# A fused attention, mixture-of-experts and gated product kernel: the last stage's token pairs taken from neighbouring columns, and its first operands formed during the last experts

## The chip, the cores and the metric

The kernel runs on one core of a Trainium2 chip. The metric is the time of one execution on the device in microseconds (us), and the time given is the median of several runs. The engines are named as in the profile: PE is TensorE (matmuls), ACT is ScalarE, DVE is VectorE, POOL is GpSimd, and SP is SyncE, which here only issues DMAs.

## The reference

The weights of the last stage are float64 in memory; tokens are the 4 x 448 = 1792 rows of `x`, with 768 features.

```python
# attention, 4 x 12 heads of 448 x 64, with q and k normalised
x = attn_out.transpose(0, 2, 1, 3).reshape(1792, 768)
# experts: each token goes to the one expert (of 8) with the largest logit
h = np.maximum(x[mask] @ w1[e], 0.0)           # 768 -> 1024
out[mask] = gate_w[mask, None] * (h @ w2[e])   # 1024 -> 768
# gated product
a = x @ moe2_w1                                # 768 -> 1024
b = x @ moe2_w2
h = a * b @ w3                                 # 1024 -> 1024
return h @ w_out                               # 1024 -> 768
```

## The kernel before

**Attention and routing** come first, to about 455 us of the span. The product of `w3` and `w_out` is formed there too. The tokens are then scattered in the order of their experts to `bk` in DRAM by POOL's indirect DMAs, seven for `bk` and fourteen small ones for `md`.

**Experts.** The eight experts run one after the other, the one with the most tokens first (room for `CAP` = 320, 288, 272, 256, 240, 224, 208, 192 tokens). SP reads each expert's number into a register (`value_load`, L781), then issues the loads of its weights (`st`, L666 and L672) and tokens (`xr` for the first expert, `xte` for the others). ACT and DVE split each weight block into an fp16 high part and an fp16 rest (`split`, L659 and L660: `w1t`, `w2t`), and PE multiplies in three terms (`mm3`, L683: high by high, low by high, high by low). Results go to columns of `y32`, six blocks of 128 features by token, three by DVE (`result`, L720) and three by ACT (L722), at a column that comes from a register. Ahead of expert 5 (`LR`) stands a loop for tokens beyond `CAP` (`overflow`, L771), which is not entered here but is a branch on every engine.

**Gated product.** `a` and `b` (called z = 0 and 1) are formed by a seven-product form of a 2 x 2 block multiplication. One of the two splits is over tokens: a column c1 of `y32` is paired with a column c2. The features split into blocks 0 to 2 and 3 to 5, which gives the four parts b11, b21, b12, b22 of the tokens. From them come seven operands, B11, B21, B22 and the differences T1 to T4, each split in two fp16 parts (`operands`, L856 on ACT and L857 on DVE, tile `b`). The tokens are treated in two pieces (s = 0, 1) of two times 448 columns: c1 = s*448, c2 = 896 + s*448. The differences go to temporaries (`t`, L868 to L875), on DVE for s = 0 and on POOL for s = 1.

The weights have seven combinations too (`combos`): for each of four column groups fp, z and three blocks j, a DMA, three DVE instructions that make fp32 of float64 (`from64`, L124 to L126, tile `y32w`), four sums on POOL (L821 to L824) and a split on ACT and DVE (`m2w`, L659 and L660). The sets (0,0), (0,1) and (1,0) of (fp, z) are written ahead of `operands(0)`. `half(fp, s)` issues 2 x 7 products of nine matmuls each for one column group and piece; in all 1008 matmuls. DVE adds up the results (L907, L909, tiles `u`, `ua`, `ub`, `c`), DVE and POOL multiply a by b, and ACT and POOL split the product into `ab`.

**Last product and scatter.** `ab` times the product of `w3` and `w_out` (L983, tile `pso`, 672 matmuls of 384 columns), then a scatter to `out` by POOL.

The order on each engine comes from a scheduler that simulates the program, from the order in which it is written; an instruction waits for its inputs and for its tile to come free, and everything behind it on its engine waits with it.

Of the kernel before, what the change touches and what calls it, by code (L numbers as in the profile page):

```python
# [44 lines left out]
def fused_kernel(ctx, tc, q, k, v, g_q, g_k, w_gate, w1, w2, m_w1, m_w2, m_w3, m_wo, out):  # L45
# [603 lines left out]
    mid = ctx.enter_context(ExitStack())  # L649
    stg = pools(mid)("stg", STG)  # L650
    xtp = pools(mid)("xtp", 2)
    w2p = pools(mid)("w2p", 9)
    ext = pools(mid)("ext", 1)
    htp = pools(mid)("htp", 2)
    ycv = pools(mid)("ycv", 2)
    y32 = yp.tile([P, 6, NT + CW], F32, name="y32")
# [76 lines left out]
    def expert(xt, w, ca, cd):  # L733
        n = xt.shape[2]
        ht = htp.tile([P, 8, 2, CW], F16, tag="ht", name="ht")[:, :, :, 0:n]
# [42 lines left out]

    for r in range(NE):
# [12 lines left out]
        if r == LR:  # L792
            overflow()
        with ExitStack() as order:
            if r < IAR:
                order.enter_context(tc.issue_after(marks["xt"].ins))
            wb += blk
        if r:
            ca = nc.scalar.value_load(srti[0:1, 2, r:r + 1], min_val=0, max_val=NT)
            cd = nc.vector.value_load(srti[0:1, 2, r:r + 1], min_val=0, max_val=NT)  # L800
        expert(xt, wb, ca, cd)
# [4 lines left out]
    HT = NT // 2  # L806
    SN = HT // 2
    SB = 4

    def combos(fp, z, j, staging, conv):  # L810
# [5 lines left out]
        y = conv.tile([P, 8, P], U32, tag="y", name="y32w")  # L816
# [17 lines left out]
    for fp, z in ((0, 0), (0, 1), (1, 0)):  # L834
        weights(fp, z, stg, ycv)
    mid.close()
    two = ctx.enter_context(ExitStack())
    bp = pools(two)("bp", 1)
    tp = pools(two)("tp", 8)
    prep2 = two.enter_context(ExitStack())  # L840
    dst = pools(prep2)("dst", 2)
    ycv2 = pools(prep2)("ycv2", 2)
    S1, S2, S3, S4, A12, A22, A11 = range(7)
    T1, T2, T3, T4, B11, B21, B22 = range(7)
    bt = [[bp.tile([P, 2, HT], F16, name=f"b{o}_{j}") for j in range(3)] for o in range(7)]

    def temp(name):
        return tp.tile([P, SN], F32, tag="t", name=name)

    def operands(s):  # L850

        c1, c2 = slice(s * SN, (s + 1) * SN), slice(HT + s * SN, HT + (s + 1) * SN)
        tt = nc.vector.tensor_tensor

        def put(o, j, x):
            nc.scalar.activation(bt[o][j][:, 0, c1], x, AF.Copy)  # L856
            tt(bt[o][j][:, 1, c1], x, bt[o][j][:, 0, c1], op=ALU.subtract)  # L857

        for j in range(3):
            put(B11, j, y32[:, j, c1])  # L860
        for j in range(3):
            put(B21, j, y32[:, j + 3, c1])
        e = tt if s == 0 else nc.gpsimd.tensor_tensor
        last = []
        for j in range(3):
            b11, b21, b12, b22 = y32[:, j, c1], y32[:, j + 3, c1], y32[:, j, c2], y32[:, j + 3, c2]
            t1, t2 = temp("t1"), temp("t2")
            e(t1, b12, b11, op=ALU.subtract)  # L868
            e(t2, b22, t1, op=ALU.subtract)
            put(T2, j, t2)  # L870
            put(T1, j, t1)
            e(t2, b21, t2, op=ALU.subtract)
            put(T4, j, t2)
            t3 = temp("t3")
            e(t3, b22, b12, op=ALU.subtract)  # L875
            put(T3, j, t3)
            put(B22, j, b22)

    def product(ps, w, a, o, s, first, last=True):
        cs = slice(a * P, (a + 1) * P)  # L880
        c1 = slice(s * SN, (s + 1) * SN)
        mm3(ps, [(w[j][:, 0, cs], w[j][:, 1, cs], bt[o][j][:, 0, c1], bt[o][j][:, 1, c1]) for j in range(3)], first, last,
            skip_group_check=not first)

    ab = []

    def half(fp, s):

        stt, tt = nc.vector.scalar_tensor_tensor, nc.vector.tensor_tensor
        c1, c2 = slice(s * SN, (s + 1) * SN), slice(HT + s * SN, HT + (s + 1) * SN)  # L890
        r = 1.0 / 256
        u = [temp("ua"), None]
# [3 lines left out]
        def begin(z):  # L896
            ps = bank(SN)
            product(ps, wst2[fp, z], A11, B11, s, True, True)
            if z:
                u[1] = temp("ub")  # L900
# [10 lines left out]
        def rest(z):  # L911
            w = wst2[fp, z]
            ps = bank(SN)
            product(ps, w, S2, T2, s, True, True)
            add(u[z], ps, u[z], z)
            ps = bank(SN)
            product(ps, w, S3, T3, s, True, True)
            t1 = temp("u3")
            add(t1, ps, u[z], z)
            product(ps, w, A22, T4, s, False, True)  # L920
            x21 = temp("c21")
            add(x21, ps, u[z], z)
            ps = bank(SN)
# [12 lines left out]
        a11 = temp("a11")  # L936
# [3 lines left out]
        yield  # L940
        done(0, 0, a11)
        a = rest(0)
        b = rest(1)
        for k in ((1, 0), (1, 1), (0, 1)):
# [4 lines left out]
    operands(0)  # L949
    h = half(0, 0)  # L950
    next(h)
    operands(1)
# [4 lines left out]
    for f in range(8):  # L957
        ab.append(abp.tile([P, 2, NT], F16, name=f"ab{f}"))
    next(h)
    for fp in range(SB):  # L960
        for s in range(2):
# [3 lines left out]
            if s == 0 and fp < SB - 1:  # L965
                weights(fp + 1, 1, dst, ycv2)
            if s == 0 and fp < SB - 2:
                weights(fp + 2, 0, dst, ycv2)
# [6 lines left out]
    order = (0, 1, 2, 7, 8, 9, 3, 4, 5, 6, 10, 11, 12, 13)  # L975
    for col in order:
# [35 lines left out]
```

## Time and profile before

| what | value |
|---|---|
| median of 3 runs | 1105.84 us (1104.05 to 1112.1) |
| profiled execution | 1105.45 us |
| its span | 1103.4 us |
| mean granted TensorE clock | 0.922 of full speed |
| PE, DVE, ACT, POOL busy | 84%, 58%, 41%, 36% of the span |

The span is what the trace covers, from the first instruction to the last; the execution's time is 2 us longer. A clock of 1.00 means the higher of TensorE's two levels, 2.4 GHz, and 0.50 the lower, 1.2 GHz. "Busy" counts only the time in which an engine executes; the busy share of PE hides whether a matmul ran at the full or the half clock.

### The profile page before, as it was taken

To read this page: it belongs to the slowest core of one execution; us is meant where nothing else is said; L and a number is where in the kernel's file an instruction comes from. 1 tells how busy PE (TensorE), PEld (TensorE's weight loads), DVE (VectorE), ACT (ScalarE), POOL (GpSimd) and SP (SyncE) were. 2 spreads that over 40 slices of the span, in tenths; PEclk is the share of its full clock that TensorE was granted. 3 is DMA by queue.
4 is the path that set the end of the run, shared out by engine and by line. 5 is a ranking of instruction groups with operands and counts; after the bars stand their busy time and mean duration, and the time that the engine had idled before them with its cause. 6 is when DMAs were issued, how large, how long until landed. Compare 5 with 4: busy or idle time off the path is not lost. (4 is left out here: it accounts for less than half of the span.)

```text
span 1103.4 us, 19950 instructions
## 1 busy us (share of the span) xinstructions
PE 932.0 (84%) x7963; PEld 616.1 (56%) x7963; DVE 637.4 (58%) x952; ACT 447.2 (41%) x651; POOL 392.7 (36%) x530
## 2 busy tenths in 40 slices
PE   1657899998878879539999998893869999999997
PEld 1224466555545557317778898893425555556664
DVE  5948647677846872247554564768975776420000
ACT  3435546576736661035443454642622232210000
POOL 6826244445552441510000000015575665431111
PEclk9876699999979989859999999997869999999999
DMA  6775454333243664368666747861111211121111
GB/s 183 250 243 157 112 118 105 96 89 88 52 147 93 166 153 99 129 210 254 229 182 179 236 159 214 289 227 61 39 39 39 77 58 39 43 72 43 58 46 56
DMA packets 159569, 141.56 MB, mean 128 GB/s; under 512 B 93344, under 2 KB 137904, under 8 KB 159472
## 3 DMA queue, kind: packets, MB, share of 16 engines
q1 hardware_dynamic: 152256, 126.06, 40.1%
q0 software_dynamic: 2864, 11.04, 2.6%
q10 hardware_dynamic: 4352, 3.15, 0.9%
q8 instruction: 63, 1.03, 0.4%
q14 instruction: 34, 0.28, 0.1%
HBM read 98.28 MB, written 22.03 MB: 109 GB/s over the span
## 5 line engine op out<-in xcount | busy, mean ns | idle before, releaser
L683 PE MATMUL psm<-b,m2w 128*128 128x448 f16 x1008 | 201.0, 362 | 32.1 <-ACT b L856 20.4
L683 PEld LDWEIGHTS <-m2w 128*128 128x128 f16 x1008 | 100.4, 100 | 132.1 <-issue 41.4
L683 PE MATMUL psm<-ht,w2t 128*128 128x320 f16 (+7 forms) x1152 | 127.8, 272 | 7.3 <-DVE ht L715 3.9
L683 PE MATMUL psm<-xte,w1t 128*128 128x320 f16 (+7 forms) x1152 | 126.3, 272 | 2.4 <-PEq L771 2.4
L683 PEld LDWEIGHTS <-w2t 128*128 128x128 f16 x1152 | 110.2, 99 | 23.6 <-issue 9.2
L683 PEld LDWEIGHTS <-w1t 128*128 128x128 f16 x1152 | 109.7, 99 | 17.8 <-issue 2.6
L821 POOL TENSOR_TENSOR y32w<-y32w 128x128 f32<-128x128 f32 x24 | 14.2, 592 | 289.6 <-DVE y32w L126 286.7
L288 DVE TENSOR_REDUCE nm<-psm 128x2 f16<-128x896 f32 x84 | 90.7, 1083 | 36.5 <-PE psm L287 36.1
L983 PE MATMUL pso<-ww,ab 128*128 128x384 f16 x672 | 109.7, 326 | 0.0
L336 PE MATMUL po<-vf,e 128*128 128x65 f32 (+1 forms) x480 | 90.8, 288 | 2.7 <-issue 2.7
L983 PEld LDWEIGHTS <-ab 128*128 128x128 f16 x672 | 65.8, 98 | 43.6
L660 DVE SCALAR_TENSOR_TENSOR w2t<-st,w2t 128x768 f16<-128x768 f32 x64 | 60.2, 955 | 47.7 <-ACT w2t L659 47.4
L287 PE MATMUL psm<-kh,qh 64*64 64x448 f16 x336 | 55.4, 409 | 31.7 <-DVE nm L288 19.6
L339 PE MATMUL po<-v,e 128*128 128x65 f16 (+1 forms) x528 | 77.9, 200 | 4.5 <-DVE x L350 2.6
L341 PE MATMUL po<-v,e 128*128 128x65 f16 (+1 forms) x528 | 76.8, 196 | 2.1 <-issue 2.1
L340 PE MATMUL po<-vl,e 128*128 128x64 f16 (+1 forms) x528 | 77.5, 197 | 1.2 <-issue 1.2
L336 PEld LDWEIGHTS po<-vf,e 128*128 128x128 f32 (+1 forms) x480 | 67.9, 191 | 11.4 <-issue 10.8
L339 PEld LDWEIGHTS <-e 128*128 128x128 f16 (+1 forms) x528 | 59.6, 118 | 22.7 <-issue 14.8
L660 DVE SCALAR_TENSOR_TENSOR w1t<-st,w1t 128x1024 f16<-128x1024 f32 x48 | 58.1, 1222 | 22.1 <-ACT w1t L659 21.9
L317 ACT ACTIVATE pss<-pss,ln 128x896 f32<-128x896 f32 x54 | 52.7, 977 | 44.0 <-PE pss L308 38.2
L659 ACT ACTIVATE w2t<-st 128x768 f16<-128x768 f32 x64 | 52.0, 838 | 37.7 <-DMA st<-in_moe_w_dram 33.2
L987 DVE TENSOR_SCALAR ob<-pso,meta_s 128x384 f32<-128x384 f32 x14 | 8.7, 618 | 98.2 <-PE pso L983 98.2
(232 smaller groups left out, 1745.4 us busy)
## 6 DMA issues: line engine op xcount, KB each, us to landing
st<-in_moe_w_dram SPq DMA_DIRECT2D x48, 512.0 KB, 4.9
st<-in_moe_w_dram SPq DMA_DIRECT2D x64, 384.0 KB, 4.0
st<-in_moe_w_dram SPq DMA_DIRECT2D x48, 256.0 KB, 3.4
w<-in_moe_w_dram SPq DMA_DIRECT2D x16, 512.0 KB, 4.0
bk<-zero SPq DMA_DIRECT2D x8, 960.0 KB, 11.6
w<-in_moe_w_out_dram SPq DMA_DIRECT2D x16, 384.0 KB, 3.6
xrow<-rx SPq DMA_DIRECT2D x12, 448.0 KB, 4.5
kf<-in_k_dram SPq DMA_DIRECT2D x24, 192.0 KB, 3.1
```

Of the source, the lines that this page charges most:

```text
L287: nc.tensor.matmul(ps[h, z, 0:S], lhsT=s["q"][0][h, c:c + 64], rhs=s["k"][0][h, S * j:S * j + S], start=True, stop=True)
L288: nc.vector.tensor_reduce(s["nm"][:, t], ps[:, :, 0:S], axis=AX.X, op=ALU.max, negate=True)
L317: nc.scalar.activation(p, p, AF.Exp, bias=ln16, scale=SCL)
L336: nc.tensor.matmul(ov[r, t, :], lhsT=e[0], rhs=vfs[i % 2][:, h, c, 0:D + 1], start=z == 0, stop=z == 3)
L339: nc.tensor.matmul(ov[r, t, :], lhsT=e[0], rhs=vh, start=z == 0, stop=False)
L340: nc.tensor.matmul(ov[r, t, 0:D], lhsT=e[0], rhs=s["vl"][:, h, c, :], start=False, stop=False)
L341: nc.tensor.matmul(ov[r, t, :], lhsT=e[1], rhs=vh, start=False, stop=z == 3)
L659: nc.scalar.activation(dst[:, 0], src, AF.Copy, scale=scale)
L660: nc.vector.scalar_tensor_tensor(dst[:, 1], src, scale, dst[:, 0], op0=ALU.mult, op1=ALU.subtract)
L683: nc.tensor.matmul(ps, lhsT=x, rhs=y, start=first and j == 0, stop=last and j == n - 1, **kw)
L821: e(s1, a21, a22, op=ALU.add)
L983: nc.tensor.matmul(pp[z], lhsT=ab[f][:, x, ts], rhs=ww[f][:, y, z * 384:(z + 1) * 384], start=f == 0 and x == 0 and y == 0, stop=f == 7 an ...
```

## The change

**Token pairs.** The pieces are now `PC = ((0, 384), (768, 512))`: piece 0 pairs columns 0 to 383 with 384 to 767, piece 1 pairs columns 768 to 1279 with 1280 to 1791. The first piece so needs only the tokens of the first experts.

**Operands.** `operands(s)` works on three feature blocks at once (3 x 384 or 3 x 512 elements), with one tile for each operand. The differences are made in place in `y32`, all on DVE. It is a generator: four steps of `operands(0)` are written behind expert 5 and the others behind expert 6, and `operands(1)` is stepped between the products of `half(0, 0)`.

**Weights.** Only the sets (0,0) and (0,1) are written ahead of the gated product. (1,0) and all later ones put their fp32 combinations into the `ab` tiles 3 and 7, which are not yet needed; j = 0 and j = 2 of a set share tile 3. Two of the first six use a token tile (`y32x`).

**Other.** Experts 5, 6 and 7 have all six results on ACT. Pools are moved, `w2p` has 8 buffers, not 9. The products of a and b of half (0, 0) come behind all its matmuls. The last product goes through the columns in order.

The core of the diff:

```diff
+    two = ctx.enter_context(ExitStack())
+    hts = [two.enter_context(ExitStack())]
+    ext = pools(hts[0])("ext", 1)
+    htp = pools(hts[0])("htp", 2)
...
-    w2p = pools(mid)("w2p", 9)
...
-    ycv = pools(mid)("ycv", 2)
+    ycv = pools(mid)("ycv", 1)
+    w2p = pools(mid)("w2p", 8)
...
-        if d % 2:
+        if d % 2 and cd is not None:
...
+    PC = ((0, 384), (768, 512))
...
+    def halves(s):
+        c, n = PC[s]
+        return slice(c, c + n), slice(c + n, c + 2 * n)
+
+    def operands(s):
+
+        c1, c2 = halves(s)
+        b11, b21, b12, b22 = y32[:, 0:3, c1], y32[:, 3:6, c1], y32[:, 0:3, c2], y32[:, 3:6, c2]
+        tt = nc.vector.tensor_tensor
+
+        def put(o, x):
+            nc.scalar.activation(bt[s][o][:, 0], x, AF.Copy)
+            tt(bt[s][o][:, 1], x, bt[s][o][:, 0], op=ALU.subtract)
+
+        put(B11, b11)
+        yield
...
+        tt(b12, b12, b11, op=ALU.subtract)
+        put(T1, b12)
+        yield
+        tt(b22, b22, b12, op=ALU.subtract)
+        put(T2, b22)
+        yield
...
+    early = operands(0)
     for r in range(NE):
...
         if r == LR:
             overflow()
+            hts.pop().close()
+            bp.append(pools(two)("bp0", 1))
+            bt.append([bp[0].tile([P, 2, 3, PC[0][1]], F16, name=f"b0_{o}") for o in range(7)])
+            hts.append(two.enter_context(ExitStack()))
+            htp = pools(hts[0])("htp2", 2)
...
-            cd = nc.vector.value_load(srti[0:1, 2, r:r + 1], min_val=0, max_val=NT)
-        expert(xt, wb, ca, cd)
+            cd = nc.vector.value_load(srti[0:1, 2, r:r + 1], min_val=low, max_val=NT) if r < LR else None
+        expert(xt, wb, ca, cd, CW if r < LR else CAP[LR])
+        for _ in range(4 if r == LR else 8 if r == LR + 1 else 0):
+            next(early, None)
...
-        y = conv.tile([P, 8, P], U32, tag="y", name="y32w")
+        if conv is ycv and (3 * z + j) % 2:
+            y = xtp.tile([P, 12, CW], F16, tag="xt", name="y32x").rearrange("p a b -> p (a b)").bitcast(U32)[:, 0:8 * P]
...
+        elif conv is None:
+            y = ab[3 + 4 * (j % 2)].rearrange("p a b -> p (a b)").bitcast(U32)[:, 0:8 * P]
...
-    for fp, z in ((0, 0), (0, 1), (1, 0)):
-        weights(fp, z, stg, ycv)
+    for z in range(2):
+        weights(0, z, stg, ycv)
+    for _ in early:
+        pass
...
+        next(steps, None)
...
-    operands(0)
+    steps = operands(1)
     h = half(0, 0)
     next(h)
-    operands(1)
+    for _ in steps:
+        pass
...
     next(h)
+    weights(1, 0, dst, None)
...
-                weights(fp + 1, 1, dst, ycv2)
+                weights(fp + 1, 1, dst, None)
```

On the engines the order moves at three places that matter. On SP at the start of the experts, the queue before reads the last of its eight registers and then issues the first weights:

```order
L781 TENSOR_LOAD srti
L781 ISA x2
L666 ISA
L666 DMA st_5987<-in_moe_w_dram 128x1024
L666 ISA
L666 DMA st_5992<-in_moe_w_dram 128x1024
```

In the changed kernel the first register is followed by the first expert's four weight loads, and the others come behind:

```order
L824 TENSOR_LOAD srti
L824 ISA x2
L670 ISA
L670 DMA st_5987<-in_moe_w_dram 128x1024
L670 ISA
L670 DMA st_5992<-in_moe_w_dram 128x1024
L670 ISA
L670 DMA st_5997<-in_moe_w_dram 128x1024
L670 ISA
L670 DMA st_6002<-in_moe_w_dram 128x1024
L824 TENSOR_LOAD srti
L824 ISA x2
```

Seven register reads moved behind the four weight loads; the tokens `xr` come behind all of them in both. On DVE behind the branch of `overflow`, before, the split of the first hidden block of expert 5 (L715) and of its second weight blocks (L660):

```order
L771 UNCONDITIONAL_BRANCH x2
L715 SCALAR_TENSOR_TENSOR ht<-psm,ht 128x224
L660 SCALAR_TENSOR_TENSOR w2t<-st_8689,w2t 128x768
L660 SCALAR_TENSOR_TENSOR w2t<-st_8694,w2t 128x768
L715 SCALAR_TENSOR_TENSOR ht<-psm,ht 128x224
L660 SCALAR_TENSOR_TENSOR w2t<-st_8699,w2t 128x768
L715 SCALAR_TENSOR_TENSOR ht<-psm,ht 128x224
L660 SCALAR_TENSOR_TENSOR w2t<-st_8704,w2t 128x768
L715 SCALAR_TENSOR_TENSOR ht<-psm,ht 128x224 x2
```

and in the changed kernel:

```order
L775 UNCONDITIONAL_BRANCH x2
L808 TENSOR_TENSOR y_5977<-y_5977 128x3x384
L800 TENSOR_TENSOR b_4_8698<-y_5977,b_4_8698 128x1152
L800 TENSOR_TENSOR b_5_8699<-y_5977,b_5_8699 128x1152
L800 TENSOR_TENSOR b_6_8700<-y_5977,b_6_8700 128x1152
L800 TENSOR_TENSOR b_0_8694<-y_5977,b_0_8694 128x1152
L719 SCALAR_TENSOR_TENSOR ht<-psm,ht 128x224
L811 TENSOR_TENSOR y_5977<-y_5977 128x3x384
L664 SCALAR_TENSOR_TENSOR w2t<-st_8704,w2t 128x768
L664 SCALAR_TENSOR_TENSOR w2t<-st_8709,w2t 128x768
L719 SCALAR_TENSOR_TENSOR ht<-psm,ht 128x224
L664 SCALAR_TENSOR_TENSOR w2t<-st_8714,w2t 128x768
```

The differences and splits of piece 0 (`b`, in place in `y_5977`, which is `y32`) stand ahead of expert 5's first hidden block and among its weight splits; the rest of them, down to the seventh, stand ahead of expert 6's weight splits. The third place is DVE around the last results of expert 7 (L720). Before, the differences of piece 0 to temporaries and the weights of the sets (0,1) and (1,0):

```order
L720 TENSOR_SCALAR y_5977<-psm 128x192
L868 TENSOR_TENSOR t_10099<-y_5977 128x448
L126 SCALAR_TENSOR_TENSOR y32w<-st_9992,y32w 128x512
L869 TENSOR_TENSOR t_10100<-y_5977,t_10099 128x448
L875 TENSOR_TENSOR t_10110<-y_5977 128x448
L868 TENSOR_TENSOR t_10116<-y_5977 128x448
L660 SCALAR_TENSOR_TENSOR m2w<-y32w,m2w 128x896
L869 TENSOR_TENSOR t_10117<-y_5977,t_10116 128x448
L875 TENSOR_TENSOR t_10127<-y_5977 128x448
L868 TENSOR_TENSOR t_10133<-y_5977 128x448
L124 TENSOR_SCALAR y32w<-st_10006 128x512
```

and in the changed kernel at the last weights of the sets (0,0) and (0,1):

```order
L664 SCALAR_TENSOR_TENSOR m2w<-y32w,m2w 128x896
L664 SCALAR_TENSOR_TENSOR m2w<-y32x,m2w 128x896
L124 TENSOR_SCALAR y32w<-st_9984 128x512
L125 SCALAR_TENSOR_TENSOR y32w<-st_9984,y32w 128x512
L126 SCALAR_TENSOR_TENSOR y32w<-st_9984,y32w 128x512
L800 TENSOR_TENSOR b_4_10024<-y_5977,b_4_10024 128x1536
L800 TENSOR_TENSOR b_5_10025<-y_5977,b_5_10025 128x1536
L800 TENSOR_TENSOR b_0_10020<-y_5977,b_0_10020 128x1536
L800 TENSOR_TENSOR b_6_10026<-y_5977,b_6_10026 128x1536
L664 SCALAR_TENSOR_TENSOR m2w<-y32w,m2w 128x896
L664 SCALAR_TENSOR_TENSOR m2w<-y32x,m2w 128x896
L811 TENSOR_TENSOR y_5977<-y_5977 128x3x512
```

The last two `m2w` splits, which are of set (0,1), stand behind four splits of piece 1's operands, 1536 elements each. The seven operands of piece 0 stand further up, behind the branch, and no result of expert 7 is on DVE.

## Rows read from the trace of the kernel before

**Rows 1.** Windows: busy us by engine with instruction counts, granted clock, DMA share, GB/s.

```profile
754.20:774.50 20.30, 0.00 (x0) 0.00 (x0) 17.88 (x27) 4.62 (x8) 11.42 (x16) 0.55 0.08 26
774.50:798.30 23.80, 23.51 (x108) 11.12 (x107) 23.80 (x38) 17.48 (x36) 14.17 (x7) 0.88 0.14 45
798.30:821.00 22.70, 11.78 (x30) 4.03 (x31) 21.20 (x25) 5.79 (x11) 18.87 (x18) 0.55 0.14 46
821.00:983.50 162.50, 161.94 (x855) 83.57 (x854) 90.75 (x133) 39.94 (x64) 84.47 (x101) 1.00 0.15 49
754.20:989.40 235.20, 203.13 (x1025) 102.00 (x1025) 154.90 (x223) 68.41 (x118) 132.19 (x145) 0.91 0.14 47
840.00:860.00 20.00, 20.00 (x107) 10.37 (x106) 16.07 (x22) 6.41 (x10) 12.14 (x15) 1.00 0.17 53
680.00:700.00 20.00, 19.17 (x203) 19.01 (x201) 13.86 (x17) 11.98 (x18) 0.00 (x0) 1.00 0.95 281
700.00:720.00 20.00, 16.93 (x168) 15.91 (x166) 14.86 (x22) 13.29 (x21) 0.00 (x0) 0.91 0.87 294
1000.00:1020.00 20.00, 20.00 (x125) 12.04 (x124) 1.85 (x3) 1.74 (x3) 2.31 (x3) 1.00 0.10 40
```

**Rows 2.** PE's waits from 755 to 990 us: total, times, longest.

```profile
PE psm L683 <- ACT b L856: 20.4, 1, 20.4
PE psm L683 <- DVE b L857: 5.9, 4, 2.6
```

**Rows 3.** PE's timeline at the first expert: start, us, instructions, idle before and releaser.

```profile
487.48 1.04 PE L703 MATMUL psm<-ident,xr 128*128 128x128 f16 x8 [32.10 <-DMA xr<-bk]
```

**Rows 4.** DVE's timeline around the start of the gated product, columns as in Rows 3.

```profile
751.86 1.17 DVE L660 SCALAR_TENSOR_TENSOR m2w<-y32w,m2w 128x896 f16<-128x896 f32 x1 [1.86 <-ACT m2w L659]
...
764.68 1.08 DVE L660 SCALAR_TENSOR_TENSOR m2w<-y32w,m2w 128x896 f16<-128x896 f32 x1
...
779.94 1.69 DVE L857 TENSOR_TENSOR b<-t,b 128x448 f16<-128x448 f32 x3
```

**Rows 5.** DVE's splits on the operand tile: duration min/median/max ns, first and last start.

```profile
L857 DVE TENSOR_TENSOR b<-y,b x18: 612/617/1551, 775.7 to 795.3; 128x448 f16<-128x448 f32 x18
```

**Rows 6.** Page, costliest groups: splits of 768 elements, busy us and mean ns.

```profile
L660 DVE SCALAR_TENSOR_TENSOR w2t<-st,w2t 128x768 f16<-128x768 f32 x64 | 60.2, 955 | 47.7 <-ACT w2t L659 47.4
...
L659 ACT ACTIVATE w2t<-st 128x768 f16<-128x768 f32 x64 | 52.0, 838 | 37.7 <-DMA st<-in_moe_w_dram 33.2
```

**Rows 7.** ACT's copies of 896 elements, tile of the weight combinations.

```profile
L659 ACT ACTIVATE m2w<-y32w x24: 933/950/952, 742.8 to 945.6; 128x896 f16<-128x896 f32 x24
```

**Rows 8.** POOL's timeline: two differences of the second piece.

```profile
786.59 8.28 POOL L868 TENSOR_TENSOR t<-y 128x448 f32<-128x448 f32 x1 [7.59 <-DVE b L857]
794.95 1.40 POOL L869 TENSOR_TENSOR t<-y,t 128x448 f32<-128x448 f32 x1
```

**Rows 9.** DVE's timeline in the steady stretch of the gated product.

```profile
843.65 1.25 DVE L124 TENSOR_SCALAR y32w<-st 128x512 uint32<-128x512 uint32 x1
...
850.41 0.61 DVE L909 SCALAR_TENSOR_TENSOR ua<-psm,ua 128x448 f32<-128x448 f32 x1
854.85 1.34 DVE L660 SCALAR_TENSOR_TENSOR m2w<-y32w,m2w 128x896 f16<-128x896 f32 x1 [3.83 <-ACT m2w L659]
```

**Rows 10.** DVE's evictions of expert results.

```profile
L720 DVE TENSOR_SCALAR y<-psm x24: 345/415/492, 522.5 to 757.2; 128x320 f32<-128x320 f32 x3, 128x288 f32 x3, 128x272 f32 x3, 128x256 f32 x3
```

**Rows 11.** PE's timeline in expert 5: its two products.

```profile
668.87 13.96 PE L683 MATMUL psm<-xte,w1t 128*128 128x224 f16 x144 [2.37 <-PEq L771]
682.66 3.13 PE L683 MATMUL psm<-ht,w2t 128*128 128x224 f16 x31
```

**Rows 12.** SP's register reads at the start of the experts.

```profile
L781 SPq TENSOR_LOAD <-srti x8: 7/698/840, 451.9 to 471.8; - x8
...
L781 SPq SEQ_ASSERT  x8: 13/379/727, 453.1 to 475.3; - x8
```

**Rows 13.** SP's timeline: the loads of the first expert's tokens.

```profile
480.34 1.78 SPq L698 DMA_DIRECT2D xr<-bk  x3
```

More of the change, by code (lines that the diff above doesn't have):

```diff
@@ L731, in hpair, with expert @@
         return ht[:, kb, 0], ht[:, kb, 1]
-    def expert(xt, w, ca, cd):
+    def expert(xt, w, ca, cd, hw=CW):
         n = xt.shape[2]
-        ht = htp.tile([P, 8, 2, CW], F16, tag="ht", name="ht")[:, :, :, 0:n]
+        ht = htp.tile([P, 8, 2, hw], F16, tag="ht", name="ht")[:, :, :, 0:n]
         for f in range(8):
@@ L777, in overflow @@
             expert_by_block(load_xt(ex, first, XW), expert_blocks(ex, "x", bufs=1), ca, cd)
+    PC = ((0, 384), (768, 512))
+    S1, S2, S3, S4, A12, A22, A11 = range(7)
+    T1, T2, T3, T4, B11, B21, B22 = range(7)
+    bp, bt = [], []
+    def halves(s):
[10 more added lines that the diff above has]
+        yield
+        put(B21, b21)
+        yield
+        put(B22, b22)
+        yield
+        tt(b12, b12, b11, op=ALU.subtract)
+        put(T1, b12)
+        yield
+        tt(b22, b22, b12, op=ALU.subtract)
+        put(T2, b22)
+        yield
+        tt(b12, b22, b11, op=ALU.subtract)
+        put(T3, b12)
+        yield
+        tt(b21, b21, b22, op=ALU.subtract)
+        put(T4, b21)
+        yield
+    early = operands(0)
     for r in range(NE):
@@ L832, in weights @@
         wst2[fp, z] = [combos(fp, z, j, staging, conv) for j in range(3)]
-    for fp, z in ((0, 0), (0, 1), (1, 0)):
-        weights(fp, z, stg, ycv)
+    for z in range(2):
+        weights(0, z, stg, ycv)
+    for _ in early:
+        pass
     mid.close()
-    two = ctx.enter_context(ExitStack())
-    bp = pools(two)("bp", 1)
-    tp = pools(two)("tp", 8)
+    hts.pop().close()
+    bp.append(pools(two)("bp1", 1))
+    bt.append([bp[1].tile([P, 2, 3, PC[1][1]], F16, name=f"b1_{o}") for o in range(7)])
@@ L840, in fused_kernel @@
+    ab0p = pools(two)("ab0p", 1)
     prep2 = two.enter_context(ExitStack())
     dst = pools(prep2)("dst", 2)
[L842 to L877, printed above, removed]
@@ L879, in product, with temp @@
+    tp = pools(prep2)("tp", 8)
+    def temp(name, s):
+        return tp.tile([P, PC[1][1]], F32, tag="t", name=name)[:, 0:PC[s][1]]
     def product(ps, w, a, o, s, first, last=True):
         cs = slice(a * P, (a + 1) * P)
-        c1 = slice(s * SN, (s + 1) * SN)
-        mm3(ps, [(w[j][:, 0, cs], w[j][:, 1, cs], bt[o][j][:, 0, c1], bt[o][j][:, 1, c1]) for j in range(3)], first, last,
+        mm3(ps, [(w[j][:, 0, cs], w[j][:, 1, cs], bt[s][o][:, 0, j], bt[s][o][:, 1, j]) for j in range(3)], first, last,
@@ L956, in fused_kernel @@
     tc.swap_default_side()
-    for f in range(8):
+    for f in range(1, 8):
         ab.append(abp.tile([P, 2, NT], F16, name=f"ab{f}"))
     next(h)
+    weights(1, 0, dst, None)
     for fp in range(SB):
@@ L974, in fused_kernel @@
         nc.sync.dma_start(ww[f].rearrange("p a b -> p (a b)"), wd[f * P:(f + 1) * P, :])
-    order = (0, 1, 2, 7, 8, 9, 3, 4, 5, 6, 10, 11, 12, 13)
-    for col in order:
+    for col in range(2 * TP):
         ts = slice(col * P, (col + 1) * P)
```

41 lines of the change are left out of this document (23 added, 18 removed).

## The prediction, made before the changed kernel was run

> **What bounds the kernel now.** I read the windows of the gated product first, since the change is aimed there [rows 1]. The stretch from the last expert's last matmul to the last of the 1008 is 235.2 us (754.2 to 989.4). In its steady part PE does 107 matmuls of 448 columns in 20 us, 0.187 each, at clock 1.00; 1008 of them are 188.4 us. The other 17 of the 1025 are of the last product, 0.160 each by the window at 1000 (125 in 20 us): 2.7. So 44.1 us are lost, and the windows say where: 20.3 with no matmul at all, then 23.8 - 108 x 0.187 = 3.6, then 22.7 - 30 x 0.187 = 17.1, then 2.7 in the 162 us that follow, and 0.4 in the rest.
>
> Next the waits [rows 2]. The first loss is one wait of 20.4 us for ACT's copy of an operand (L856), and 5.9 more go to DVE's split of one (L857). From 774.5 to 821 DVE is busy nearly throughout (100% to 798.3): it makes operands, adds up results and converts weights, and PE, far from its rate, falls to a granted clock of 0.55, near the lower level. Behind 821 the product runs at its rate. The loss is one of the beginning, paid once.
>
> Of the rest, PE's 32.1 us wait ahead of the first expert [rows 3] concerns the change by one queue, SP's. The last product keeps its instructions.
>
> **The change part by part.** The sum is made against the profiled execution, 1105.45 us (span 1103.4 and 2 around it); the median of the three runs, 1105.84, is 0.4 off, which I neglect.
>
> *Matmuls.* Half of the 1008 have 384 columns, half 512: the mean stays 448. 384 columns take 0.160 us and 448 take 0.187 [rows 1], in proportion to the columns, so no price per matmul shows. 188.4 us stay.
>
> *Start gap, 20.3 before.* Piece 0's operands stand behind the branch of the overflow loop, some 80 us early. PE then needs only the weights (0,0), and the third of these splits ended at 753.0 already [rows 4]. I take 1.5 us (0 to 5).
>
> *Weights (0,1).* The order gives PE 48 matmuls of 384 columns that need (0,0) and the first block of (0,1): 48 x 0.160 = 7.7 us, to about 763.4. The last two splits of (0,1) stand behind four splits of 1536 elements. An operation with two inputs takes 0.61 us for 448 elements [rows 5] and 1.08 for 896 [rows 4], so 0.00105 per further element; three of 448 in a row take 1.69 [rows 4], so 0.07 of each overlaps the next. That gives 1.28 us for 1152 and 1.68 for 1536. Four are 6.7 us; ACT's copies ahead of them, 0.838 at 768 and 0.950 at 896 [rows 6, 7], come to 1.51 and keep pace. From 756, when ACT has evicted expert 7's last result and done the first copy, DVE is through at 763, and the two weight splits end at about 765: PE waits 2 us. But the sums for these weights are on POOL, and one POOL difference that met a row of DVE's splits took 8.28 us, the next 1.40 [rows 8]. Were the sums held off for all of the four splits, 6.7 us would be added. I take 5 for this wait (1 to 9).
>
> The Trainium skill, page SBUF — State Buffer, section "SBUF: two separate sides", says that GpSimd and a VectorE operation with two SBUF inputs take one port pair as an exclusive lock, so that the loser waits for a whole instruction. The 8.28 us agree in kind, but it is more than one instruction of the splits next to it. By that rule alone each of eight sums could wait for a long split or hold one up, and the estimate for this wait would be its upper end, 9, and the whole 4 us longer.
>
> *Rest of piece 1's operands.* Three differences and three splits on DVE, 6 x 1.68 = 10.1, and about eight evictions of 0.61 [rows 9], 4.9: 15 us from 765 to 780. In that time PE has the rest of the first half, 78 x 0.160 = 12.5 us, and the first products of piece 1, as far as PSUM banks are free. I take 4 us lost (0 to 10; the upper end is a bit over half of what the like stretch from 798 to 821 lost).
>
> *Later weights.* (1,0) starts only when the `ab` tiles can be written, behind the last use of `y32` at about 779. In the steady stretch two conversions in flight take 12.5 us (843.65 to 856.2) [rows 9]. Tile 3 has two a set: (1,0) is done at about 799 and (1,1) at about 819. PE has both halves of group 0, 126 x 0.160 + 126 x 0.213 = 47 us, and reaches group 1 at 754 + 47 + 10 = 811. (1,0) is hidden by that work, (1,1) is some us late for the end of the first products. I take 4 (0 to 14).
>
> *Clock.* Before, the 20 us pause came ahead of the low rates [rows 1]. Without it I take 1.5 us for matmuls at half clock around the short waits (0 to 4).
>
> These add up to 1.5 + 5 + 4 + 4 + 1.5 = 16 us in place of 44.1: 28.1 gained.
>
> *Experts 5 and 6.* DVE gets 4 differences and 7 splits of 1152, 11 x 1.28 = 14.1 us, and loses nine evictions of expert results, 9 x 0.38 = 3.4 (between the least and the median of [rows 10]). ACT gets seven copies of 1.17 and the nine evictions, 11.6. From 680 to 720 DVE is busy 28.7 of 40 us, ACT 25.3, and the DMAs 0.95 and 0.87 [rows 1]: there is room, and the weights come at DMA's pace. But in expert 5 the last hidden block (L719) stands behind ten of the long ones: 12.8 + 8 x 0.38 + 7 weight splits of 0.96 [rows 6] = 22.6 us from the branch at 669, to about 692, where the second product began at 682.7 [rows 11]. PE has 80 of its 144 matmuls, 8 us, ahead of the first that needs that block, so it is late by 1 to 2, and part of the 3.1 us that PE lost from 700 to 720 gives it back. I take +1.5 (-2 to +8). SP's queue has the transpose of expert 6's tokens ahead of its weights; it is in that range.
>
> *Start of the experts.* SP's eight register reads, with their checks, go from 451.9 to 475.3, 2.9 us a set [rows 12]; then come the weights and, at 480.34, `xr` [rows 13], for which PE waits [rows 3]. With the four weight loads ahead of seven of the reads, their time falls into the reads' or delays them: `xr` at about 478. I take -2.3 (-4 to +1.5, the latter if the reads are simply pushed back by the loads less their gap).
>
> *Other edits.* Eight `w2p` buffers, not nine, make a split wait for a block of the expert before, which is freed one block (1.8 us) later; the row of hidden blocks covers it. The column order of the last product moves nothing that PE waits for. Both at nothing, within the range.
>
> The sum: -28.1 + 1.5 - 2.3 = -28.9, so **1076.5 us**.
>
> **Rivals.**
> *DVE becomes the bound in the first pair of halves.* From 754 DVE has 11 x 1.68 = 18.5 us for piece 1's operands, 28 evictions, some 17, the six conversions of (1,0) and (1,1), 6 x 2.9 = 17 (three operations of 512 elements and one of 896, by the figures above), and 4 of the set before: 57 us against PE's 47. For it speaks that DVE was full from 774.5 to 798.3; against it that POOL's differences, which slowed it, are gone. If POOL costs it another 10 to 12, 25 of the 44 us stay lost: 1085.5.
>
> *The experts are pushed.* If expert 5's weights and hidden blocks are late as well as expert 6's, +10 in place of +1.5: 1085. Against it speaks the room in the windows.
>
> *Piece 0's operands don't come early.* If a tile frees late and holds their copies, the splits slide behind expert 7. The gap is then 20 again and the wait for (0,1) is hidden: 1076.5 + 18.5 - 5 = 1090, and up to 1095 with DVE's pile-up.
>
> *Slower: the conversion chain through tile 3.* Before, two tiles rotated for the combinations; now j = 0 and j = 2 of a set share one, twelve conversions one behind the other from 779 on. Their last is needed at about 754 + 16 + 3 x 47 + 5 = 916: 11.4 us each are free. At 12.5, the time of a pair in flight, the last comes at 929, 13 late: 1089. From 13.9 each it eats the whole gain, and at 15, when each waits in DVE's and POOL's queues between evictions, it ends at 959, 43 late: 1119. Against it: a conversion's own work on DVE and ACT is 2.9 + 0.95 us, and the 12.5 cover two.
>
> **How the numbers follow.** The forecast has 0.65, DVE as the bound 0.17, the pushed experts 0.07, operands not early 0.03, the slow chain 0.04 and a gain beyond 1064 (the short waits near their lower ends) 0.04. The range 1064 to 1090 leaves out the last two, the upper half of the third rival and the forecast's own tail, together about 0.15. A measurement of this kernel can tell about 1%, 11 us. Faster by more than that, under 1095: forecast, the first two rivals and the large gain, less a tail of 0.02: 0.91. Within it, this tail and the third rival: 0.05. Slower, the chain: 0.04.
>
> **What would show it.** PE's timeline should have a matmul on an operand within 5 us of the last expert's end, then a pause of some us that names `m2w` or its split, and in the 70 us from there a sum of losses near 16, against 41 before; clock near 1.00. The splits of 1152 should lie from 669 to 695, and expert 6 should start within 3 us of its old distance from expert 5. `xr` should be issued some 2 us earlier. I would be wrong if the splits of piece 0 wait for something behind the branch, if PE's waits for `m2w` recur behind 830, or if DVE is full to 830.

## The result and the profile after

| | before | changed |
|---|---|---|
| median of 4 runs | 1107.34 us | 1074.17 us (1072.1 to 1076.79) |
| ratio, 95% interval | | 0.9699 (0.9655 to 0.9742) |
| profiled execution | 1105.45 us | 1076.79 us |
| its span | 1103.4 us | 1075.1 us |

The change makes the kernel 3.0% faster: 33.2 us by the medians, 28.7 us between the two profiled executions. 1076.5 us had been predicted for the latter. Windows of the changed kernel, in the columns of [rows 1], split where its own waits lie:

```profile
752.44:769.10 16.66, 10.65 (x54) 5.16 (x52) 13.40 (x12) 10.05 (x12) 11.39 (x11) 0.90 0.01 1
769.10:806.40 37.30, 37.15 (x191) 18.66 (x192) 32.32 (x38) 11.44 (x16) 14.22 (x19) 1.00 0.22 71
806.40:820.00 13.60, 9.94 (x45) 4.79 (x45) 11.60 (x16) 3.95 (x6) 10.93 (x13) 0.87 0.24 78
820.00:961.10 141.10, 139.99 (x739) 72.03 (x737) 78.23 (x115) 32.94 (x53) 74.31 (x94) 1.00 0.18 59
752.44:961.10 208.66, 197.73 (x1027) 100.65 (x1026) 135.54 (x178) 58.38 (x86) 110.85 (x136) 0.98 0.18 58
```

The stretch from the last expert's end to the last of the 1008 takes 208.7 us, where [rows 1] has 235.2. With 188.4 for the matmuls at their rate and 15 of the last product (2.4), 17.9 us are lost, not 44.1; 16 had been predicted. DVE is no longer full, and the clock is at 1.00 from 769 to 806, where [rows 1] has 0.55 behind 798.

PE's waits in this stretch, as in [rows 2]:

```profile
PE psm L687 <- DVE u L935: 4.8, 2, 3.7
PE psm L687 <- ACT m2w L663: 4.3, 2, 2.9
PE psm L687 <- DVE m2w L664: 1.7, 3, 0.9
```

The 20.4 us for an operand are gone. What is left is 10.8 us: evictions (`u`, L935) and weights (`m2w`), no operand at all. PE's timeline, in the columns of [rows 3], shows where:

```profile
680.17 13.96 PE L687 MATMUL psm<-ht,w2t 128*128 128x224 f16 x144
...
743.37 9.23 PE L687 MATMUL psm<-ht,w2t 128*128 128x192 f16 x110 [0.94 <-ACT ht L718]
752.44 1.14 PE L687 MATMUL psm<-b,m2w 128*128 128x384 f16 x6
754.98 0.34 PE L687 MATMUL psm<-b,m2w 128*128 128x384 f16 x1 [1.40 <-ACT m2w L663]
...
767.99 0.82 PE L687 MATMUL psm<-b,m2w 128*128 128x384 f16 x4 [2.94 <-ACT m2w L663]
...
810.06 50.16 PE L687 MATMUL psm<-b,m2w 128*128 128x512 f16 x255 [3.67 <-DVE u L935]
```

PE goes from the last expert's product to the first on `b` without a pause (743.37 + 9.23 is 752.6, and the row of the matmuls behind starts at 752.44). It stops after six, for ACT's copy of the third block of (0,0), then 2.94 us at 765 for (0,1), then 3.67 at 806 for an eviction (the 255 matmuls of the last row are those up to 860, where the view ends). The second product of expert 5 (680.17) runs in one piece: the long splits ahead of the hidden blocks cost it nothing.

DVE's timeline, as in [rows 4]:

```profile
667.46 5.16 DVE L800 TENSOR_TENSOR b<-y,b 128x1152 f16<-128x1152 f32 x4 [0.63 <-ACT b L799]
...
687.05 0.38 DVE L719 SCALAR_TENSOR_TENSOR ht<-psm,ht 128x224 f16<-128x224 f32 x1
...
759.10 7.54 DVE L800 TENSOR_TENSOR b<-y,b 128x1536 f16<-128x1536 f32 x4
...
803.79 0.43 DVE L124 TENSOR_SCALAR ab<-st 128x512 uint32<-128x512 uint32 x1 [2.53 <-DMA st<-in_moe_w_dram]
...
810.04 0.69 DVE L935 TENSOR_TENSOR u<-psm,u 128x512 f32<-128x512 f32 x1
```

Four splits of 1152 take 5.16 us (1.29 each; 1.28 estimated), and expert 5's last hidden block is in at 687.05, 5 us earlier than I had it. The four splits of 1536 take 7.54, not 6.7. The reason is in POOL's timeline, as in [rows 8]:

```profile
754.30 0.46 POOL L878 TENSOR_TENSOR y32x<-y32x 128x128 f32<-128x128 f32 x1
...
759.32 1.84 POOL L877 TENSOR_TENSOR y32w<-y32w 128x128 f32<-128x128 f32 x1 [2.88 <-DVE y32w L126]
761.13 1.97 POOL L878 TENSOR_TENSOR y32w<-y32w 128x128 f32<-128x128 f32 x1
763.05 1.97 POOL L879 TENSOR_TENSOR y32w<-y32w 128x128 f32<-128x128 f32 x1
765.10 1.85 POOL L880 TENSOR_TENSOR y32w<-y32w 128x128 f32<-128x128 f32 x1
```

A sum of 128 elements takes 0.46 us when DVE leaves it alone (754.30), and 1.84 to 1.97 while DVE makes these splits. By these times POOL and DVE go turn by turn, four sums (759.32 to 766.95) to four splits (759.10 to 766.64). So the last sum ends at 766.95 and PE gets (0,1) at 768.

At the start of the experts, SP's timeline as in [rows 13] and PE's as in [rows 3]:

```profile
455.06 9.39 SPq L670 DMA_DIRECT2D st<-in_moe_w_dram  x4
480.36 1.76 SPq L702 DMA_DIRECT2D xr<-bk  x3
```

```profile
483.54 1.03 PE L707 MATMUL psm<-ident,xr 128*128 128x128 f16 x8 [27.00 <-DMA xr<-bk]
```

The four weight loads now start at 455.06, but `xr` is issued at 480.36, as before (480.34). It lands 3.1 us later, not 7.1.

### The profile page after: what moved, and what is told of

It is laid out like the page before. It is cut to its first block, busy times and chain, and to the rows that moved or that the text cites. A ratio compares the mean times of both kernels' runs of the same rounds, so it can differ in the third digit from the quotient of the medians.

```text
span 1075.1 us, 19872 instructions
## 1 busy us (share of the span) xinstructions
PE 925.3 (86%) x7963; PEld 612.6 (57%) x7963; DVE 631.8 (59%) x911; ACT 444.3 (41%) x632; POOL 372.5 (35%) x518
## 5 line engine op out<-in xcount | busy, mean ns | idle before, releaser
L687 PE MATMUL psm<-b,m2w 128*128 128x384 f16 (+1 forms) x1008 | 195.6, 356 | 10.9 <-DVE u L935 4.8
L877 POOL TENSOR_TENSOR y32w<-y32w 128x128 f32<-128x128 f32 x3 | 3.4, 1127 | 264.6 <-DVE y32w L126 264.6
L319 DVE TENSOR_TENSOR e<-pss,e 128x896 f16<-128x896 f32 x54 | 58.4, 1082 | 10.7 <-ACT e L318 10.7
```

The source lines that it names most:

```text
L319: nc.vector.tensor_tensor(b, p, a, op=ALU.subtract)
L687: nc.tensor.matmul(ps, lhsT=x, rhs=y, start=first and j == 0, stop=last and j == n - 1, **kw)
```

## The experiments

The runs were made in three series: e1 to e4, e5 to e8, e9 to e12. In the first two both kernels take some 14 us less than at first, nearly all of it ahead of the first expert; in the third they take what they took at first. The record gives the second and the third series the same chip number, so that the chip makes this difference is not shown, though some of the expectations say so. Ratios are against the kernel before in the same series. The changed kernel run again (e5, in the second series) is the one to compare e1 to e7 with; for e1 to e4 this is a comparison of ratios from two series.

**e1, the bound undone.** `low` is the least column that an expert's results may have. At 0, an expert's results may lie anywhere in `y32` as far as the program knows, so operands made there in place and the results of the last experts have to wait for each other. The run also takes out the early steps, so it shows what early operands are worth, not what the bound does alone.

```diff
-            low = r * NT // NE
+            low = 0
...
-        for _ in range(4 if r == LR else 8 if r == LR + 1 else 0):
-            next(early, None)
```

> The changed kernel with one bound undone: the columns that experts 5 to 7 may write start at 0 again, as before, in place of r*NT/NE, and the early steps are taken out of the experts' loop. Pairs of neighbouring columns, three blocks at once, the later (1,0) weights and all else stay. Theory (what the change gives is that piece 0's operands exist when the last expert ends): the operands come behind expert 7, PE's gap ahead of the gated product is 12 to 22 us again, the time 1086 to 1098 us. Rival (fewer and longer operations and the moved weights give it, wherever the operands stand): at most 1079 us.

Ratio 0.985 (0.981 to 0.989), 14.6 us over the changed kernel by the two ratios. PE's timeline, and POOL's:

```profile
748.99 0.49 PE L687 MATMUL psm<-b,m2w 128*128 128x384 f16 x2
753.36 2.74 PE L687 MATMUL psm<-b,m2w 128*128 128x384 f16 x10 [3.88 <-ACT m2w L663]
771.73 0.50 PE L687 MATMUL psm<-b,m2w 128*128 128x384 f16 x1 [15.63 <-ACT m2w L663]
```

```profile
764.57 4.77 POOL L875 TENSOR_TENSOR y32w<-y32w 128x128 f32<-128x128 f32 x1 [7.51 <-DVE y32w L126]
769.31 0.45 POOL L876 TENSOR_TENSOR y32w<-y32w 128x128 f32<-128x128 f32 x1
```

The range of 1086 to 1098 was made for the times of the first measurement; over its 1107 it is 0.981 to 0.992, and 0.985 lies in it. In the time the theory holds and the rival falls: without early operands about half of the gain is gone. (The profiled execution, 1085.82 us, is 8.7 us over the median of its runs, 1077.17. Its stretch of the gated product takes 221 us against 208.6 in e5, so most of the loss lies there.) But the gap that was expected, 12 to 22 us ahead of the first product, did not come: PE starts at 748.99 without a pause, and its long wait, 15.6 us, is for weights, not for an operand. The splits of both pieces stand in one row on DVE, among the conversions of the last weights, and one sum on POOL takes 4.77 us among them, the next 0.45. Late operands cost time here by what they put ahead of the weights in DVE's queue.

**e2, pairs half a range apart again, with the bound.**

```diff
-    PC = ((0, 384), (768, 512))
+    PC = ((0, 440), (440, 456))
...
-        return slice(c, c + n), slice(c + n, c + 2 * n)
+        return slice(c, c + n), slice(NT // 2 + c, NT // 2 + c + n)
```

> The changed kernel with tokens paired half a range apart again (440 columns from 0 with those from 896, and 456 from 440 with those from 1336), all else kept, the bound on the experts' columns too. Theory (the pairs only matter through what the first piece waits for; with the bound it needs the results of expert 5, not of 6 and 7): the splits move from expert 5 into expert 6, the gap stays under 3 us, the time within 5 us of the changed kernel, 1070 to 1079 us. Rival (neighbouring pairs are what makes it possible): the gap is 10 us or more, the time over 1084 us.

Ratio 0.9723 (0.9682 to 0.9765), the changed kernel's within the interval. PE's timeline:

```profile
737.97 1.28 PE L687 MATMUL psm<-b,m2w 128*128 128x440 f16 x6
740.63 0.36 PE L687 MATMUL psm<-b,m2w 128*128 128x440 f16 x1 [1.38 <-ACT m2w L663]
...
752.94 0.92 PE L687 MATMUL psm<-b,m2w 128*128 128x440 f16 x4 [3.68 <-ACT m2w L663]
```

There is no gap at 738, and the waits for weights are those of the changed kernel. (The 1070 to 1079 of the expectation is again in the times of the first measurement; the ratio is what it asks for.) That the paired columns are neighbours is worth nothing that these runs can tell; the first piece has only to be free of the last experts, here 6 and 7.

**e3, the long splits of piece 1 cut in three.**

```diff
-            tt(bt[s][o][:, 1], x, bt[s][o][:, 0], op=ALU.subtract)
+            for k in range(3) if s else (slice(0, 3),):
+                tt(bt[s][o][:, 1, k], x[:, k], bt[s][o][:, 0, k], op=ALU.subtract)
```

> The changed kernel with each split of 1536 elements on DVE cut into three of 512, in the same place of the order; nothing else. Theory (a DVE operation with two inputs and a POOL operation shut each other out for a whole operation): POOL's four sums among these splits fall from 1.9 us each to about 1.0, the weights (0,1) are ready 2 to 3 us earlier on ACT, PE's wait for them falls from 3.2 to 1.5 us or less, and the time by 1 to 2 us, less some 0.5 us for 14 further operations. Rival (POOL gets a share of the port by DVE's elements, however they are cut): the sums stay at 1.8 to 1.9 us each and the time is the same or 0.5 to 1 us longer.

Ratio 0.9696 (0.9662 to 0.973), not to be told from the changed kernel's. POOL's timeline during the splits, and DVE's:

```profile
740.46 0.77 POOL L878 TENSOR_TENSOR y32w<-y32w 128x128 f32<-128x128 f32 x1 [2.88 <-DVE y32w L126]
741.19 0.90 POOL L879 TENSOR_TENSOR y32w<-y32w 128x128 f32<-128x128 f32 x1
742.05 0.90 POOL L880 TENSOR_TENSOR y32w<-y32w 128x128 f32<-128x128 f32 x1
743.03 0.78 POOL L881 TENSOR_TENSOR y32w<-y32w 128x128 f32<-128x128 f32 x1
```

```profile
740.23 8.35 DVE L801 TENSOR_TENSOR b<-y,b 128x512 f16<-128x512 f32 x12
748.50 1.08 DVE L664 SCALAR_TENSOR_TENSOR m2w<-y32w,m2w 128x896 f16<-128x896 f32 x1
```

The sums take 0.77 to 0.90 us instead of 1.84 to 1.97, with the same elements on DVE: each sum waits for a whole operation of DVE, and the shorter that is, the shorter the wait. A share by elements, the rival, would have left them at 1.8 to 1.9. The four are through 3.4 us after the first began (740.46 to 743.81), where it was 7.6. PE's wait fell by less than I expected, 3.2 to 2.4: the weight splits stand behind all twelve pieces on DVE's queue (748.50).

**e4, three buffers for the later weights' loads.**

```diff
-    dst = pools(prep2)("dst", 2)
+    dst = pools(prep2)("dst", 3)
```

> The changed kernel with three buffers, not two, for the loads of the later weights; nothing else. Theory (PE's wait of 3.7 us at 806 and the 1.1 us at 889 come from a conversion that stands in DVE's queue waiting for its load, 2.5 and 3.5 us, with evictions of PSUM behind it): DVE no longer waits for these loads there, both waits of PE go, and the time falls by 3 to 5 us. Rival (DVE is full in that stretch and the evictions would be late anyway): the waits only change their name, the time is within 1 us.

Ratio 0.9679 (0.9649 to 0.9709), 4.0 us under e5 by the ratios, though the intervals overlap. PE's waits behind 770, where the changed kernel has 4.8 us for `u`:

```profile
PE psm L687 <- DVE u L935: 1.3, 1, 1.3
```

With 1.0 us for others that is 2.3 us in place of 4.8 (3.4 in e5), and the stretch is 205.5 us long, not 208.6. So most of the wait at 806 came from the load: in DVE's rows above the conversion at 803.79 starts the moment its load is in, and the evictions for which PE waits come behind it, at 810.04. Not all of it: in e4 no conversion waits for a load there, and 1.3 us of this wait stay, where the theory had none. The wait of 1.1 us at 889 is gone.

**e5, the changed kernel again.**

> The changed kernel as it is, beside the others of this call: the reference for them. Against the kernel before its ratio should be 0.970 within the interval of the first measurement, 0.9655 to 0.9742, also on a chip whose times are shorter by some 14 us on both.

Ratio 0.9716 (0.9686 to 0.9746), as expected. The stretch of the gated product takes 208.6 us here, too.

**e6 and e7, two buffers for the first combinations, alone and with e4's edit.**

```diff
-    ycv = pools(mid)("ycv", 1)
+    ycv = pools(mid)("ycv", 2)
```

> The changed kernel with two buffers, as before, for the fp32 combinations of the first weights (y32w) in place of one; nothing else. By the order, all six splits of (0,0) and (0,1) then stand on DVE ahead of piece 1's splits. Theory (PE's 2.8 us for the last block of (0,0) and 3.2 for (0,1) come from sums and splits that stand behind piece 1's long operations on DVE): both waits fall to 2 us together or less, piece 1's operands come some 5 us later without being waited for by more than 2, and the time falls by 2 to 4 us against the changed kernel. Rival (DVE has just so much to do until 785, and what is moved up is waited for elsewhere): PE's waits up to 815 add up as before, the time is within 1 us.

Of the first six combinations three have the tile `y32w` and three, not two as said of the change, a token tile (`y32x`). Ratio 0.9709 (0.9682 to 0.9736): the same as e5. PE's timeline, then DVE's and POOL's at the later weights:

```profile
742.67 0.50 PE L687 MATMUL psm<-b,m2w 128*128 128x384 f16 x2 [1.79 <-DVE m2w L664]
744.83 42.66 PE L687 MATMUL psm<-b,m2w 128*128 128x384 f16 x226 [1.66 <-ACT m2w L663]
...
805.09 73.52 PE L687 MATMUL psm<-b,m2w 128*128 128x384 f16 x382 [8.29 <-ACT m2w L663]
```

```profile
788.79 0.43 DVE L124 TENSOR_SCALAR ab<-st 128x512 uint32<-128x512 uint32 x1 [2.15 <-DMA st<-in_moe_w_dram]
```

```profile
802.49 1.15 POOL L961 TENSOR_TENSOR ab<-ua,ab 128x512 f16<-128x512 f32 x1
803.60 0.45 POOL L880 TENSOR_TENSOR ab<-ab 128x128 f32<-128x128 f32 x1
```

The waits for (0,0) and (0,1) fall from 6.0 to 3.5 us, less than the theory asked for, but PE runs on to 787 without another. Then it waits 8.3 us, 797 to 805, for weights of group 1. Their conversion was late for want of its load (DVE waits 2.15 us for it), and their last sum then stood behind the half's products and splits in POOL's queue, to 803.60. By the times the rival holds for this edit alone: nothing is gained. The trace is of the slowest of its five runs, 1067.69 us against a median of 1061.52, and its stretch takes 213.2 us, 4.6 more than e5's. So it shows where what was gained can be lost again, but 8.3 us can't be the loss in the median run, whose time is e5's.

> The changed kernel with both: two buffers for the first combinations and three for the loads of the later weights. Theory: the two waits are separate, at 752 to 769 and at 806, so the gains add: 4 to 8 us under the changed kernel. Rival (one pile-up of DVE's work, seen at two places): no better than the better of the two alone.

Ratio 0.9661 (0.9631 to 0.9692), 6.0 us under e5. The window of its stretch:

```profile
738.63:939.30 200.67, 194.41 (x1028) 99.78 (x1026) 132.35 (x174) 56.85 (x83) 108.62 (x132) 1.00 0.19 60
```

200.7 us, 7.9 under e5's and 4.8 under e4's. The theory's 4 to 8 holds in the time and in the trace. Against e4, the better of the two alone, the time is only 2.0 us less by the ratios, well within their intervals, so the times don't exclude the rival. That the loads' third buffer is what lets the earlier weights count fits e6, which alone gave nothing, but rests on single traces.

**e8, the first expert's tokens ahead of its weights, in the kernel before.**

```diff
-WFIRST = 4
+WFIRST = 0
```

> The kernel before with the loads of the first expert's tokens (xr) issued ahead of its four weight loads in place of behind them; nothing else. Theory (xr landed 3.1 us after its issue in the changed kernel and 7.1 before, because the 2 MB of weights no longer stood just ahead of it in the DMA queues): xr lands about 3 us after its issue, which is 2 to 3 us earlier, PE's first work on it starts 5 to 7 us earlier against SP's last register read; then the first expert waits for its weights, and what stays of it is 0 to 3 us. Rival (the prediction's: the issue sets it, the landing does not depend on the queue): xr still takes about 7 us to land.

Ratio 0.9944 (0.992 to 0.9967), 6.1 us, more than the 0 to 3 expected. SP's timeline and PE's:

```profile
454.60 1.74 SPq L698 DMA_DIRECT2D xr<-bk  x3
```

```profile
461.33 1.03 PE L703 MATMUL psm<-ident,xr 128*128 128x128 f16 x8 [10.71 <-DMA xr<-bk]
...
468.03 7.55 PE L683 MATMUL psm<-xte,w1t 128*128 128x320 f16 x35 [1.59 <-ACT w1t L659]
```

`xr` takes 7.4 to 7.8 us to land with nothing of SP's just ahead of it, as the rival has it. But in this series SP reaches the loads while POOL's scatters still run (to 468), and in e5, too, where the weights were issued 12 us ahead of it, `xr` needs 6.8 to 8.5. So this run doesn't decide what the weights ahead of it cost; it shows only that this order is the better one for the kernel before in this series. Of the kernel before no trace was taken in it, so where the 6.1 us lie is open.

**e9, the kernel before again.** No edit.

> The kernel before as it is, for its profile on the chip of these runs: on it the times of both kernels are some 14 us shorter than in the first measurement. Theory (the shorter time lies ahead of the experts, and the change acts on the same stretches on either chip): from expert 5's start to the last matmul on m2w it takes the time of the first trace within 2 us (320.5 us), and the gap ahead of the gated product is 20 us again.

Its time is again that of the first measurement, not that of e5 to e8, so its first aim failed. 1105.1 us; from expert 5's start to the last matmul on `m2w` 318.9 us (320.5 in the first trace), with the same wait of 20.4. `xr` landed in 6.5 us, behind four weight loads.

**e10, tokens first on top of e7.** e7's two edits and e8's.

> The changed kernel with two buffers for the first combinations, three for the later loads, and the first expert's tokens loaded ahead of its weights. Theory (the loads in the DMA queues hold each other up at the start of the experts, tokens first is the better order, as it took 6 us off the kernel before): 1 to 4 us under the kernel with the two edits alone, 0.964 or less against before. Rival (in the changed kernel the four weight loads are issued 10 us ahead of the tokens and cost them nothing, while with the tokens first the first product waits for weights): 0 to 4 us longer than the two edits alone.

Ratio 0.9637 (0.9607 to 0.9667): the lowest of all, 3.6% under the kernel before, against 3.0% of the changed kernel. By the ratios that is 2.7 us under e7, but the intervals overlap and the series differ, so whether the tokens' place adds anything to it stays open.

**e11, the later (1,0) weights alone, in the kernel before.**

```diff
-    for fp, z in ((0, 0), (0, 1), (1, 0)):
+    for fp, z in ((0, 0), (0, 1)):
...
     next(h)
+    weights(1, 0, dst, ycv2)
     for fp in range(SB):
```

> The kernel before with one part of the change alone: the weights (1,0) are written behind the first half's products, not ahead of the gated product. Theory (their conversions filled DVE and POOL around the gap and were worth part of the 44 us): PE's gap falls by 1 to 3 us and the waits behind it by 3 to 6, the time by 3 to 8 us. Rival (what is not done there is done a little later while DVE is still full): within 2 us of before.

Ratio 0.992 (0.9891 to 0.9948), 8.9 us, a little over the theory's range. PE's timeline:

```profile
753.73 10.16 PE L683 MATMUL psm<-ht,w2t 128*128 128x192 f16 x119 [1.62 <-ACT ht L714]
770.47 1.65 PE L683 MATMUL psm<-b,m2w 128*128 128x448 f16 x4 [6.58 <-ACT b L856]
...
801.85 6.15 PE L683 MATMUL psm<-b,m2w 128*128 128x448 f16 x19 [7.46 <-DVE a L939]
```

The gap falls from 20.4 to 6.6 us, much more than the 1 to 3 I gave it: with the conversions of (1,0) out of ACT's and DVE's queues, the first operand is copied 14 us earlier, counted from the last expert's end. 7.5 of them are lost at 794, where the waits behind grew; the stretch takes 224.4 us in place of 235.2.

**e12, the bound alone, in the kernel before.**

```diff
+            low = r * NT // NE
-            ca = nc.scalar.value_load(srti[0:1, 2, r:r + 1], min_val=0, max_val=NT)
-            cd = nc.vector.value_load(srti[0:1, 2, r:r + 1], min_val=0, max_val=NT)
+            ca = nc.scalar.value_load(srti[0:1, 2, r:r + 1], min_val=low, max_val=NT)
+            cd = nc.vector.value_load(srti[0:1, 2, r:r + 1], min_val=low, max_val=NT)
```

> The kernel before with one part of the change alone: the least column that an expert may write is r*NT/NE, not 0. Theory (the bound frees piece 0's operands of the last experts' results, but they have no room of their own before the experts' tiles are given back, so the order keeps them behind expert 7): the gap stays at 18 us or more, the time within 3 us of before. Rival (the bound is all that held them): the gap falls under 8 us, the time by over 10 us.

Ratio 0.9994 (0.9971 to 1.0018). PE's timeline:

```profile
775.89 22.46 PE L683 MATMUL psm<-b,m2w 128*128 128x448 f16 x108 [20.43 <-ACT b L857]
```

Nothing moves. The bound alone frees nothing. In the program the operands' tiles take the place of the experts' (the pool is opened behind them), and they are written behind expert 7; the changed kernel has the bound, a pool that is opened behind expert 4 and the early steps.

## Why the prediction was right, point by point

The sum was right within a microsecond: -28.9 predicted, -28.7 between the two profiled executions. So close a hit is luck. The profiled execution of the changed kernel is the slowest of its four, by the medians the gain is 33.2 us (28.6 to 38.2 by the interval of the ratio), and the terms are off both ways. As the prediction had them:

| term | predicted | measured | from |
|---|---|---|---|
| start gap (20.3 before) | 1.5 | 0, and 2.8 for (0,0) | PE's timeline |
| weights (0,1) | 5 | 3.2 | PE's timeline |
| rest of piece 1's operands | 4 | at most 1.0 | window 769 to 806 |
| later weights | 4 | 3.7 and 1.1, for evictions | PE's waits |
| all other, clock among it | 1.5 | 7.1 | 17.9 - 10.8 (holds the 1.0 above) |
| experts 5 to 7 | +1.5 | +0.8 | 752.44 - 666.38 against 754.15 - 668.87 |
| start of the experts | -2.3 | -2.1 | first product at 490.60 against 492.67 |

**Right, and shown.** Early operands are worth about half of the gain: with them there is no gap, and with them late (e1) 14.6 us come back, though as a wait for weights. POOL's sums are held off by long splits: the estimate of 5 us for this wait stood between 2 and 9 on the ground of one row, 8.28 us against 1.40, and e3 shows the mechanism. The Trainium skill, page SBUF — State Buffer, section "SBUF: two separate sides", describes this as an exclusive lock for a whole instruction. The turns of 1.84 to 1.97 us, and 0.77 to 0.90 with shorter splits, agree; the 4.77 of e1 and the 8.28 of [rows 8], where one POOL operation waited through several of DVE's, are more than that sentence tells. By the rule alone I had said 9; the four sums that met the splits cost PE 3.2.

**Right in sum, off in a term.** The third block of (0,0) was not ready as I read it from [rows 4]: piece 1's first difference, 2.00 us on DVE at 750.22, held up a sum of it, which took 1.97 on POOL. I had looked at the waits of (0,1) alone. The rest of piece 1's operands cost nearly nothing, since PE had enough products of piece 0. The later weights came out at the size I gave them, but not for my reason: behind 770 PE waits for no weights. Its 3.7 and 1.1 us are evictions that stood behind a conversion waiting for its load, and I had no term for the loads' two buffers. The clock and small losses, 7.1 us, were nearly five times my figure. The granted clock is 0.90 up to 769 and 0.87 from 806 to 820, each behind a pause: 2 us of the 54 matmuls to 769 (10.65 against 54 x 0.160) and 1.8 of the 45 from 806 (9.94 against 18 of 512 columns and 27 of 384, 8.16 at their rates) are such losses. About 1 us is lost from 769 to 806 (37.3 against 108 of 512 columns and 83 of 384, 36.3 at their rates) and 2 us in the 141 us behind 820, at a clock of 1.00. The prediction had counted 2.7 us of the last kind among the 44.1 of before, and has no term for what stays of them.

**Wrong in the reason.** In the term for the start of the experts, "`xr` at about 478" is wrong: it was issued at 480.36. What was gained is its landing, 3.1 us against 6.5 to 7.2 in four traces (before, e9, e11, e12) in which four weight loads stand just ahead. That the loads are the cause fits, but e8, made to show it, ran where the scatters overlap, so it is not shown.

**Missing.** The prediction let the early operands alone take away the gap. e11 shows that two thirds of it, 13.8 of 20.4 us, went with (1,0)'s conversions, which stood ahead of the copies in the queues. Their move alone is worth 8.9 us (5.8 to 12.1); I had counted only its later cost. How far this gain and that of early operands overlap no run shows. As to what makes the operands early, e2 shows that the neighbouring pairs are not needed, and e12 that the bound alone is not enough; that the bound is needed beside the room is read from the program, since no run has the room and the early steps without it.

**The rivals.** DVE is not the bound (32.3 of 37.3 us busy from 769). The experts were not pushed: expert 6 starts 27.6 us behind expert 5, where it was 28.6. The chain through tile 3 does not show as a chain: behind 820, PE waits 1.1 us in all, and with a third buffer for the loads (e4) 1.3 us are left of the wait at 806.

## What to carry to other kernels

Before an operation is moved to an early gap, look for what holds it in the program's own terms: the range that a write with a register's address is taken to cover, and the memory that its tile takes over. Giving the old kernel one of them alone, as e12 does, tells in one run whether it is enough. When DVE's long operations with two inputs meet short ones of POOL that someone waits for, put the short ones ahead, or cut the long ones; but cutting (e3) gains only as far as the queue behind is not also in the way. A wait that is removed at the front of a stretch is worth what the next limit leaves of it: two buffers for the first combinations gave nothing alone (e6).

## What was not expected of the hardware

The eight register reads of SP, with their checks, took 0.9 us a set in e8 (reads from 447.2 to 453.6) and 2.9 in the first trace (451.9 to 471.8 in [rows 12]), during POOL's scatters in both. The loads themselves hardly differ (medians 0.61 and 0.70 us); the assertions behind them take 0.02 and 0.38 us. PE's wait for `xr`, which follows them, is 16.1 to 17.0 us for the changed kernel in e1 to e7 and 27.0 in its first trace, so some 10 of the 14 us between the series lie here. What makes the pace differ is not shown. One POOL operation of 128 elements was held for 4.77 us by DVE operations in a row, although between the four splits of the changed kernel each sum had its turn.
